# Last softmax sums on TensorE, slot 1's tokens gathered during attention, and four smaller moves

## The chip, the core and the metric

The kernel runs on one NeuronCore of one Trainium2 chip. The metric is the device time of one execution, in microseconds (us). The core's engines run side by side and wait for each other through semaphores: TensorE (PE: matmuls; its weight loads are listed as PEld), VectorE (DVE), ScalarE (ACT), GpSimd (POOL), and SyncE (SP), which here only issues DMAs. POOL issues the DMAs that gather or scatter rows by an index (DMA_INDIRECT).

## What is computed

Attention with normalized q and k, and behind it a mixture of experts that sends each token to one expert. Cut to what matters:

```python
# 8 batches, 12 heads, 448 tokens, head size 64
q_n, k_n = rmsnorm(q, g_q), rmsnorm(k, g_k)
scores = (q_n @ k_n.T) / 8
attn = exp(scores - max) ; attn = attn / (sum(attn) + 1e-9)
x = (attn @ v) laid out as 3584 tokens x 768

logits = x @ w_gate + modality_bias[modality_id]      # 8 experts
e_idx = argmax(logits, axis=1)
gate_w = softmax(logits)[arange, e_idx]
for e in range(8):
    mask = e_idx == e
    h = relu(x[mask] @ w1[e])                          # 768 -> 1024
    out[mask] = gate_w[mask] * (h @ w2[e])             # 1024 -> 768
```

## The kernel before

**Attention.** The work is cut into 48 units; unit u holds two heads (h = 0, 1) of batch u // 6. A unit has seven steps j, and the counter n = 7 u + j runs from -22 (a run-in) to 335. At each step the table `PLAN` says which pieces each engine gets. The scores of step j are the matmuls `st`; ACT's exponential turns them into the tiles p[:, j]; the matmuls `av` multiply p with v. Step 3 holds both heads (64 partitions each), the steps 0 to 2 the one head, 4 to 6 the other. `avcopy` takes the finished unit out of PSUM, DVE transposes it, and it is stored to `x_d` in DRAM.

The softmax's denominators take two stages. `csum` (line 924) adds the seven p tiles of a unit into two tiles `cs`, one for each head: one SCALAR_TENSOR_TENSOR on DVE and five 128x448 additions on POOL. `sums` (line 970) then adds over the partitions with four matmuls, against a table `sel` of zeros and ones, for two units at once. `gates` multiplies the same tokens with w_gate, into the same PSUM tile `pm`, and `recips` and the routing functions pick each token's expert and its place in that expert's list. `route_put` writes the list rows to `l_d` in DRAM, one scattered DMA for each of a batch's four chunks (c = 0 to 3).

**Mixture of experts.** The lists are cut into 14 static slots of 256 tokens. A slot has 24 steps. In the first eight, 144 matmuls `ph` (line 550) multiply the slot's tokens with w1, in four groups of 36 (`ph_0` to `ph_3`); in the other sixteen, 96 matmuls `py` (line 581) do the second product. Every fp32 operand is split in a high and a low part, so each product is three matmuls. ACT casts the high part, DVE subtracts it to get the low part:

- x: POOL gathers the rows of a slot in eight DMAs (`xrw<-x_d,i`, the function `xload`); DVE scales and transposes them, in three groups (`xtr`); ACT casts (`xcp`) and DVE subtracts (`xw<-xrw,xw`);
- w1: three gathers into `r_0`, `r_1`, `r_2`, and twelve pieces (`w1w<-r,w1w` 128x512). `ph_0` wants the pieces 0, 4 and 8, `ph_1` the pieces 1, 5, 9, and so on;
- w2: four gathers into `r2w`, and four pieces (`w2lw<-r2w,w2ha` or `w2hb`);
- the hidden layer: `hhw` (ACT) and `hlw` (DVE) empty each `ph` group from PSUM. There are two PSUM tiles for `ph`, so `ph_2` can't start before `hlw` has emptied `ph_0`.

The table `MOE` gives the step for each piece; what it doesn't name stands at a step that a formula gives. Slots 0 to 2 are tabled from the lists of the first six batches and can start while the last two are still in attention; the rest are tabled (`tables2`, the small DVE operations `tb_...`, `nbp`, `nbi`) when all batches are routed. The last part of attention and the start of the experts are woven by hand: between the two halves of `ph_0` stand the last `av`, `sums` and `gates`.

Nothing reorders work at run time: each engine works through its list in the order written, and waits where a semaphore isn't there yet. Nearly all instructions are issued through the recording helper at lines 54 and 55, so those two line numbers say nothing; the tiles' names do. `xrw` and `r2w` are large buffers that several things use in turn.

Of the kernel before, what the change touches and what calls it, by code (L numbers as in the profile page):

```python
# [68 lines left out]
def kernel(  # L69
# [36 lines left out]
    wg = cp.tile([128, NP, 32], F32, name="wg")  # L106
    sel = cp.tile([128, 2, 32], F32, name="sel")
# [12 lines left out]
    V.memset(lnb[:, 1:2], -22.0 * math.log(2.0))  # L120
    V.memset(wg, 0.0)
    V.memset(sel, 0.0)
    for i in range(2):
        V.memset(sel[:, i, 16 + i : 17 + i], 1.0)

    def load_gains():
        SY.dma_start(gg[:, 0], g_q.unsqueeze(0))
        SY.dma_start(gg[:, 1], g_k.unsqueeze(0))

    def gain_product(ps):  # L130
        for i in range(2):
# [1430 lines left out]
```

## Time and profile before

| | |
|---|---|
| time, three runs | 1060.64, 1062.4, 1065.34 us (median 1062.4) |
| the profiled execution | 1063.27 us, its span 1061.5 us |
| mean granted TensorE clock | 0.977 of full |
| busy, of the span | PE 95%, PEld 75%, DVE 73%, POOL 69%, ACT 66% |
| matmuls `ph` / `py` / `st` | 255.6 / 115.0 / 175.0 us and more for other shapes |

The profiled execution lies 0.87 us above the median and 1.77 us above its own span. Attention ends at about 552 us of the span, the experts take the rest. Busy shares are means over stretches with different limits, so they don't say what any one stretch waits for.

### The profile page before, as it was taken

Reading aid. Unit: us, or ns where it says so; the run is one execution under the profiler, and the core shown is the slowest. Engines: PE = TensorE matmul, PEld = TensorE weight load, DVE = VectorE, ACT = ScalarE, POOL = GpSimd, SP = SyncE. Lnnn points to the kernel's source line nnn. Section 1 sums busy time; section 2 is a strip of 40 time slices with the busy share of each in tenths; the row PEclk is TensorE's granted clock in tenths of the full one; section 3 lists DMA queues with packets and bytes.
Section 4 is the critical chain, followed back from the end, with each engine's and each line's share of the span. In section 5 each row is a group of like instructions: output and inputs, shape, how many; then the busy total and the mean of one; then the engine's idle time right before and its main releaser. Section 6 shows DMA issues by size and latency. Waiting matters only on the chain. (4 is left out here: it accounts for less than half of the span.)

```text
span 1061.5 us, 19477 instructions
## 1 busy us (share of the span) xinstructions
PE 1006.8 (95%) x6271; PEld 800.8 (75%) x6271; DVE 778.5 (73%) x1500; ACT 698.0 (66%) x1409; POOL 729.7 (69%) x743
## 2 busy tenths in 40 slices
PE   7789999999999999998979799999999999999996
PEld 6646565665566656554549699999999999999996
DVE  7778887887888888887696786766766677566830
ACT  5668998888888888876554445545645555455630
POOL 4697877898888888887765766776556655566231
PEclk8999999999999999999989798999999999999999
DMA  6767777767677776656613112221172211121070
GB/s 178 159 185 191 189 187 189 185 168 178 173 191 187 183 186 166 163 141 154 191 48 123 50 44 46 62 65 48 35 265 76 63 32 43 49 61 45 32 256 33
DMA packets 174803, 133.30 MB, mean 126 GB/s; under 512 B 119148, under 2 KB 168400, under 8 KB 173540
## 3 DMA queue, kind: packets, MB, share of 16 engines
q1 hardware_dynamic: 150836, 90.69, 35.0%
q0 software_dynamic: 23856, 41.28, 12.2%
q8 instruction: 51, 0.84, 0.4%
q14 instruction: 60, 0.49, 0.2%
HBM read 139.06 MB, written 24.18 MB: 154 GB/s over the span
## 5 line engine op out<-in xcount | busy, mean ns | idle before, releaser
L550 PE MATMUL ph<-xw,w1w 128*128 128x256 f32 x2016 | 255.6, 289 | 9.7 <-ACT xw L54 5.5
L550 PEld LDWEIGHTS ph<-xw,w1w 128*128 128x128 f32 x2016 | 251.3, 197 | 14.7 <-ACT xw L54 6.3
L54 DVE TENSOR_REDUCE at_hlw<-sa 128x1 f32<-128x448 f32 x336 | 204.7, 613 | 78.1 <-PE sa L889 63.0
L916 PE MATMUL st<-w1w 128*128 128x448 f32 x480 | 175.0, 414 | 11.9 <-ACT at_w2lw L54 10.4
L916 PEld LDWEIGHTS st<-w1w 128*128 128x128 f32 x480 | 84.1, 191 | 102.2 <-ACT xw L54 24.9
L54 POOL DMA_INDIRECT xrw<-x_d,i x112 | 135.6, 1210 | 36.6 <-issue 30.6
L54 POOL DMA_INDIRECT r2w<-in_moe_w_dram,tb_w2i x48 | 55.9, 1164 | 107.7 <-DVE w2lw L54 101.9
L54 DVE TENSOR_TENSOR w1w<-r,w1w 128x512 fp32r<-128x512 f32 (+1 forms) x180 | 113.9, 679 | 16.2 <-ACT w1w L54 16.2
L889 PE MATMUL sa<-w1w 128*128 128x448 f32 x282 | 107.8, 384 | 10.1 <-DVE at_hlw L54 9.3
L54 ACT ACTIVATE at_w2lw<-st 128x448 f32<-128x448 f32 x168 | 89.6, 541 | 39.2 <-PE st L916 34.9
L581 PE MATMUL py<-w2lw,hhw 128*128 128x384 f32 x448 | 115.0, 334 | 0.0
L54 ACT ACTIVATE hhw<-ph 128x512 fp32r<-128x512 f32 x56 | 33.5, 598 | 119.9 <-PE ph L550 119.9
L54 ACT CAST w1w<-xw 64x448 fp32r<-64x448 f32 x188 | 105.5, 561 | 6.1 <-DVE xw L54 2.4
L54 ACT CAST w1w<-r 128x512 fp32r<-128x512 f32 (+1 forms) x180 | 102.8, 639 | 1.7 <-ACT w2hb L54 1.0
L916 PE MATMUL st<-w1w,w2ha 65*128 65x448 f32 x288 | 101.1, 371 | 1.2 <-DMA w1w<-xw 1.2
L54 ACT ACTIVATE r2w<-st 128x448 f32<-128x448 f32 x168 | 90.1, 539 | 16.5 <-PE st L916 10.7
L54 DVE TENSOR_TENSOR w2lw<-r2w,w2ha 128x1536 fp32r<-128x1536 f32 x28 | 49.2, 1758 | 67.1 <-ACT w2ha L54 63.7
L54 POOL TENSOR_TENSOR xrw<-r,at_hlw 112x512 f32<-112x512 f32 x89 | 93.6, 1053 | 5.4 <-PE tr L802 3.5
L54 POOL TENSOR_TENSOR r2w<-r2w 128x448 f32<-128x448 f32 (+1 forms) x72 | 84.2, 1170 | 15.5 <-ACT r2w L54 6.6
L54 ACT ACTIVATE yw<-py,lt 128x384 f32<-128x384 f32 x55 | 29.0, 577 | 81.7 <-issue 56.8
L581 PEld LDWEIGHTS py<-w2lw,hhw 128*128 128x128 f32 x448 | 81.0, 188 | 0.0
L889 PEld LDWEIGHTS sa<-w1w 128*128 128x128 f32 x282 | 54.0, 192 | 23.7 <-DVE at_hlw L54 18.0
(312 smaller groups left out, 2140.9 us busy)
## 6 DMA issues: line engine op xcount, KB each, us to landing
w1w<-xw SPq DMA_DIRECT2D x312, 112.0 KB
r<-in_q_dram SPq DMA_DIRECT2D x48, 224.0 KB
r<-in_k_dram SPq DMA_DIRECT2D x48, 224.0 KB
w2ha<-xw SPq DMA_DIRECT2D x72, 112.0 KB
x_d<-at_w2hb SPq DMA_DIRECT2D x8, 672.0 KB
x_d<-yw SPq DMA_DIRECT2D x8, 672.0 KB
r2w<-in_v_dram SPq DMA_DIRECT2D x24, 128.0 KB
at_w2lw<-in_v_dram SPq DMA_DIRECT2D x24, 128.0 KB
```

What stands on the lines that cost most here:

```text
L54: return fn(*a, **kw)
L550: PE.matmul(ps[:, i], lhsT=lt_, rhs=rt_[:, c], start=n == 0, stop=n == 17)
L581: PE.matmul(ps[n][:, :384], lhsT=lt_[:, j, 128 * t : 128 * t + 128], rhs=rt_[:, 384 * n : 384 * n + 384], start=j == 0 and m == 0, stop=j ...
L889: PE.matmul(ps[:, :S], lhsT=t["qq"][:, h, a : a + 128], rhs=t["kk"][h], start=True, stop=True)
L916: PE.matmul(ps[:, :S], lhsT=l, rhs=t["qq"][:, h] if first else t["ql"][:, h], start=first and (j != 3 or h == 0), stop=not first and (j != ...
```

## The change

1. **Sums.** For the units 46 and 47 `csum` is left out. A new function `psums` adds p over steps and partitions in one go, with eight matmuls a unit against a table `selw`: unit 46's in pairs between the last `st`, unit 47's where `sums` stood.
2. **Slot 1's x.** Its list rows and its eight gathers are issued in attention (n = 302, 314, 325 to 332). Its transposes move from the steps 16, 17, 19 to 8, 8, 12. Slot 2's gathers stand together at step 8 (five stood at 20, three at 32), its transposes at 26, 28, 30 (38, 40, 42). The last three units' `xt` moves out of `xrw`; for that w2's fourth piece of slot 0 is gathered at step 5, behind the last transpose.
3. **Lists.** `route_put` writes through 32 views of `l_d` that are told apart, so that the scattered writes don't wait for each other. The puts of batch 6 and 7 and the second tables (`rpos` step 14 to 8, `tab2` 21 to 9, `flush` 46 to 40) come earlier.
4. **Gate tables.** Six DMAs (w_gate in four, modality ids, bias) are issued by ACT at n = -22, no longer by SyncE at n = -2.
5. **Smaller.** `l_d` is zeroed by four DMAs (n = 8, 11, 14, 17), not eight (7 to 14); POOL's last addition for head 0 stands behind that of head 1's second (`cse`); the norms of load 4 move from n = 2 to 1, the squares of unit 6's k from 1 to 3. Many other entries of `MOE` change, most of them to what the formula gives anyway; from slot 5 on the order is the same but for one x group.

```diff
-'cse': (1, 2) ... ('sk', 6): 1 ... ('nk', 4): 2 ... 'lg': -2, 'lz': 7 ... 'x0': 28
+'cse': (2, 2) ... ('sk', 6): 3 ... ('nk', 4): 1 ... 'lg': -22, 'lz': (8, 11, 14, 17) ... 'x0': 27 ...
+ 'pj': (2, 3, 4, 6, 2, 3, 4) ... 'g1': 34, 'f1': 22, 'x1': (325, 326, 327, 328, 329, 330, 331, 332)
...
+    l_v = dram_disjoint_views(l_d[:], B * NCH)
...
-                    SY.dma_start(wg[64 * h : 64 * h + 64, i::2, 8 * h : 8 * h + 8], src[i, h ^ i])
-            SY.dma_start(modr, mod_id.bitcast(I32).rearrange("(b p w) -> p b w", b=B, p=CP))
+                    A.dma_start(wg[64 * h : 64 * h + 64, i::2, 8 * h : 8 * h + 8], src[i, h ^ i])
+            A.dma_start(modr, mod_id.bitcast(I32).rearrange("(b p w) -> p b w", b=B, p=CP))
...
-    xt_e = [view(xrw, 2 * DM + S * i, 128, S) for i in range(3)]
+    xt_e = [view(r2w, PW + VW + W, 128, S), xt_b[3], view(r2w, PW + VW + S, 128, S)]
...
+        def psums(u, js):
+            i = 2 * (u % 2)
+            for j in js:
+                for h in range(2):
+                    if j == 3 or j // 4 == h:
+                        k_ = i + (h ^ (u % 2))
+                        PE.matmul(pm[32 * k_ : 32 * k_ + 32, :S], lhsT=selh[h] if j == 3 else sel[1],
+                                  rhs=T[u]["p"][:, j], start=False, stop=False, tile_position=(0, 32 * k_))
...
-            G.indirect_dma_start(out=l_d[:], out_offset=IOFF(ap=posi[:, c : c + 1], axis=0),
+            G.indirect_dma_start(out=l_v[NCH * b + c], out_offset=IOFF(ap=posi[:, c : c + 1], axis=0),
...
-        XSTEPS = {0: ((1, 7, range(8)), (2, 17, range(5))), 1: ((2, 32, range(5, 8)),),
+        XSTEPS = {0: ((2, 8, range(8)),), 1: (),
...
+        for j in range(NJ):
+            put(NJ * (NU - 1) + P["pj"][j], "psums", NU - 2, ORD[0][j : j + 1])
...
-            if 0 <= i < NU and j in CSJ:
+            if 0 <= i < NU - 2 and j in CSJ:
...
+            if n in P["x1"]:
+                xload(1, [b_ for b_ in range(8) if P["x1"][b_] == n])
...
-                wload(0, 1)
+                wload(0, 1, (0, 1, 2))
...
+            if s == 0:
+                on(("w2", 0, 3), 5, part(wload, 0, 1, (3,)))
...
-        step(1, part(mm1_half, 0, 0, 1, p0), part(sums, u - 1), part(gates, g))
+        step(1, part(mm1_half, 0, 0, 1, p0), part(psums, u, (0, 4, 1, 5, 2, 6, 3)), part(gates, g))
```

Three places show what moves on the engines. The first is PE's list at the end of attention, from the last `av` of unit 46 to the gates; `pm` is the PSUM tile of sums and gates. Before:

```order
L916 MATMUL st_4_6332<-w1w 128x448 x2
L916 MATMUL st_2_6341<-w1w 128x448 x2
L1055 MATMUL rt_6345<-oh_6231,ones 128x32
L1056 MATMUL rt_6345<-oh_6231,tri 112x32
L916 MATMUL st_5_6354<-w1w 128x448 x2
L916 MATMUL st_6_6368<-w1w 128x448 x2
L550 MATMUL ph_0_6423<-xw,w1w 128x256 x18
L960 MATMUL av_6320<-at_w2lw 64x448 x6
L550 MATMUL ph_0_6423<-xw,w1w 128x256 x18
L975 MATMUL pm<-at_w2lw,sel 32x448 x2
L975 MATMUL pm<-at_w2hb,sel 32x448 x2
L982 MATMUL pm<-at_w2hb,wg 32x448
```

And with the change (line numbers are 5 to 15 higher):

```order
L990 MATMUL pm<-r2w,selw 32x448 x2
L921 MATMUL st_4_6356<-w1w 128x448 x2
L990 MATMUL pm<-r2w,selw 32x448 x2
L921 MATMUL st_2_6370<-w1w 128x448 x2
L990 MATMUL pm<-r2w,selw 32x448 x2
L1069 MATMUL rt_6376<-oh_6235,ones 128x32
L1070 MATMUL rt_6376<-oh_6235,tri 112x32
L921 MATMUL st_5_6384<-w1w 128x448 x2
L921 MATMUL st_6_6394<-w1w 128x448 x2
L990 MATMUL pm<-r2w,selw 32x448 x2
L555 MATMUL ph_0_6440<-xw,w1w 128x256 x18
L965 MATMUL av_6339<-at_w2lw 64x448 x6
```

Four pairs of `pm` matmuls now stand among `st` and in front of `ph_0`. Behind the second half of `ph_0`, where the two rows of `sums` stood, come the eight of unit 47:

```order
L555 MATMUL ph_0_6440<-xw,w1w 128x256 x18
L990 MATMUL pm<-at_w2lw,selw 32x448 x8
L996 MATMUL pm<-at_w2hb,wg 32x448
L996 MATMUL pm<-r2w,wg 32x448
L996 MATMUL pm<-at_w2lw,wg 32x448
L996 MATMUL pm<-r2w,wg 32x448
```

The second place is POOL's list from the last gathers of slot 0's x on: the ten additions of the units 46 and 47 before, and w2 and w1 behind them.

```order
L54 DMA xrw<-x_d,i_129 128x192 x2
L54 TENSOR_TENSOR r2w<-r2w 128x448
L54 TENSOR_TENSOR r2w<-r2w 64x448
L54 TENSOR_TENSOR at_w2lw<-r2w 128x448
L54 TENSOR_TENSOR r2w<-r2w 128x448
L54 TENSOR_TENSOR at_w2lw<-r2w 128x448
L54 TENSOR_TENSOR r2w<-at_w2lw 128x448
L54 TENSOR_TENSOR r2w<-r2w,at_w2lw 64x448
L54 TENSOR_TENSOR at_w2hb<-r2w,at_w2lw 128x448
L54 TENSOR_TENSOR r2w<-r2w,at_w2lw 128x448
L54 TENSOR_TENSOR at_w2hb<-r2w,at_w2lw 128x448
L54 DMA r2w<-in_moe_w_dram,ta_w2i 128x1536 x4
```

With the change the eight gathers of slot 1's x stand there, in one row of ten with the last two of slot 0; the row `xrw` x8 further down is slot 2's x, where slot 1's x stood before.

```order
L55 DMA xrw<-x_d,i_130 128x192 x10
L55 DMA r2w<-in_moe_w_dram,ta_w2i 128x1536 x3
L55 DMA r_0_153<-in_moe_w_dram,ta_w1i 128x2048
L55 DMA r_1_154<-in_moe_w_dram,ta_w1i 128x2048
L55 DMA l_d<-ltb,posi_6381 28672x16 x3
L55 DMA r_2_155<-in_moe_w_dram,ta_w1i 128x2048
L55 DMA r2w<-in_moe_w_dram,ta_w2i 128x1536 x3
L55 DMA xrw<-x_d,i_130 128x192 x8
L55 DMA r2w<-in_moe_w_dram,ta_w2i 128x1536 x2
```

The third place is DVE's list behind the last `hlw` of slot 0, while PE is in slot 0's `py`. Before, the w1 pieces and the placing of batch 7 (`bs`, `zb`, `px_e`) come first, and x's first group behind them:

```order
L54 TENSOR_TENSOR w1w<-r_0_152,w1w 128x2x256 x3
L54 TENSOR_TENSOR w1w<-r_1_153,w1w 128x2x256
L54 TENSOR_TENSOR w1w<-r_0_152,w1w 128x2x256
L54 TENSOR_TENSOR w1w<-r_2_154,w1w 128x2x256
L55 TENSOR_REDUCE bs_6773<-zb_119 128x40
L55 TENSOR_REDUCE zb_118<-bs_6773 128x8
L55 TENSOR_TENSOR px_e<-px_e,bs_6773 112x32
L55 TENSOR_TENSOR px_e<-px_e,oh_6570 112x32
L55 TENSOR_REDUCE px_e<-px_e 112x4
L55 CAST posi_6774<-px_e 112x4
L54 TENSOR_TENSOR xrw<-xrw,lt_128 128x8x64
L54 STREAM_TRANSPOSE xrw<-xrw 128x2x8x32
```

With the change two groups of x are scaled and transposed in front of the first w1 piece, and small operations stand between the pieces (further down those of `tables2`):

```order
L55 TENSOR_TENSOR w2lw<-r2w,w2hb 128x1536
L55 TENSOR_TENSOR xrw<-xrw,lt_129 128x8x64
L55 STREAM_TRANSPOSE xrw<-xrw 128x2x8x32
L55 TENSOR_TENSOR xrw<-xrw,lt_129 128x8x64
L55 STREAM_TRANSPOSE xrw<-xrw 128x2x8x32
L55 TENSOR_TENSOR w1w<-r_0_153,w1w 128x2x256
L56 TENSOR_REDUCE bs_6720<-zb_120 128x40
L56 TENSOR_REDUCE zb_119<-bs_6720 128x8
L56 TENSOR_TENSOR px_e<-px_e,bs_6720 112x32
L55 TENSOR_TENSOR xw<-xrw,xw 128x512 x2
L55 TENSOR_TENSOR w1w<-r_0_153,w1w 128x2x256
```

What moved: x to the front, and the small operations of the second tables from slot 1's `ph` into slot 0's `py`.

## Rows read from the trace of the kernel before

**Rows 1.** The chain that ended last, 560 to 720 us: start, length, what.

```profile
638.72 18.41 PE ph L550 x131
```

**Rows 2.** Stretches: length, busy time (x instructions) by engine, granted clock, DMA share, GB/s.

```profile
533.60:546.15 12.55, 7.46 (x36) 3.46 (x35) 11.80 (x15) 6.04 (x15) 8.01 (x7) 0.83 0.08 4
...
570.79:587.60 16.81, 16.81 (x98) 16.49 (x96) 8.94 (x17) 5.56 (x10) 13.76 (x11) 1.00 0.16 42
...
587.60:616.48 28.88, 22.50 (x145) 21.03 (x146) 24.94 (x54) 14.20 (x19) 21.79 (x18) 0.76 0.16 46
...
633.12:657.13 24.01, 21.26 (x146) 20.31 (x146) 16.03 (x22) 12.21 (x16) 13.49 (x11) 0.86 0.24 51
...
673.77:691.00 17.23, 17.23 (x145) 17.23 (x145) 12.75 (x17) 10.69 (x14) 12.84 (x11) 1.00 0.24 63
```

**Rows 3.** PE's timeline, 529 to 552 us: start, length, instruction, [idle before <-releaser].

```profile
530.34 0.55 PE L975 MATMUL pm<-at_hhw,sel 128*32 128x448 f32 x2
...
530.82 0.47 PE L916 MATMUL st<-w1w 128*128 128x448 f32 x1
...
533.61 2.48 PE L960 MATMUL av<-r2w,at_w2lw 128*64 128x448 f32 x12
...
540.62 0.68 PE L916 MATMUL st<-w1w 128*128 128x448 f32 x2 [2.40 <-ACT at_w2lw L54]
...
544.34 1.87 PE L916 MATMUL st<-w1w 128*128 128x448 f32 x4 [2.69 <-ACT at_w2lw L54]
...
546.15 2.96 PE L550 MATMUL ph<-xw,w1w 128*128 128x256 f32 x13
...
549.72 0.85 PE L550 MATMUL ph<-xw,w1w 128*128 128x256 f32 x5 [0.60 <-DVE xw L54]
```

**Rows 4.** DVE's timeline, 528 to 540 us.

```profile
529.70 0.42 DVE L54 TENSOR_TENSOR w1w<-r,w1w 128x256 fp32r<-128x256 f32 x1
...
531.22 1.88 DVE L54 TENSOR_TENSOR w1w<-r,w1w 128x256 fp32r<-128x256 f32 x1
...
533.35 1.24 DVE L54 SCALAR_TENSOR_TENSOR r2w<-r2w,half 128x448 f32<-128x448 f32 x1
...
537.07 1.63 DVE L54 TENSOR_TENSOR xrw<-xrw,lt 128x512 f32<-128x512 f32 x1
```

**Rows 5.** POOL's timeline, 528 to 538 us.

```profile
529.31 1.02 POOL L54 DMA_INDIRECT xrw<-x_d,i  x1 [0.16 <-issue]
...
531.65 2.45 POOL L54 TENSOR_TENSOR r2w<-r2w 128x448 f32<-128x448 f32 x2
```

**Rows 6.** ACT's timeline at 539 us.

```profile
539.48 0.65 ACT L54 CAST xw<-xrw 128x512 fp32r<-128x512 f32 x1 [4.46 <-DVE xrw L54]
```

**Rows 7.** DVE's timeline, 565 to 632 us.

```profile
565.89 1.72 DVE L54 TENSOR_TENSOR w2lw<-r2w,w2ha 128x1536 fp32r<-128x1536 f32 x1
...
589.13 0.69 DVE L54 TENSOR_TENSOR xrw<-xrw,lt 128x512 f32<-128x512 f32 x1 [9.26 <-DMA xrw<-x_d,i]
...
590.49 0.65 DVE L54 TENSOR_TENSOR w1w<-r,w1w 128x512 fp32r<-128x512 f32 x1
...
599.30 0.17 DVE L55 TENSOR_SCALAR nbi<-run 128x8 int32<-128x8 f32 x1
...
630.27 0.69 DVE L54 TENSOR_TENSOR xrw<-xrw,lt 128x512 f32<-128x512 f32 x1 [3.73 <-DMA xrw<-x_d,i]
```

**Rows 8.** PE's timeline, 587 to 617 us.

```profile
591.31 0.58 PE L550 MATMUL ph<-xw,w1w 128*128 128x256 f32 x1 [3.71 <-ACT xw L54]
...
598.60 18.04 PE L550 MATMUL ph<-xw,w1w 128*128 128x256 f32 x131 [0.41 <-DVE xw L54]
```

**Rows 9.** ACT's timeline at 9 us.

```profile
8.63 0.65 ACT L55 ACTIVATE at_hlw<-at_hlw,lnb 112x16 f32<-112x16 f32 x2 [4.19 <-DVE at_hlw L54]
```

**Rows 10.** SyncE's DMA queue at 36 us.

```profile
36.10 2.70 SPq L141 DMA_DIRECT2D wg<-in_moe_w_gate_dram  x4
```

**Rows 11.** POOL's timeline at 44 us.

```profile
43.90 2.28 POOL L54 TENSOR_TENSOR xrw<-xrw 112x256 f32<-112x256 f32 x5 [7.00 <-ACT xrw L54]
```

More of the change, by code (lines that the diff above doesn't have):

```diff
@@ L6 @@
 from concourse import mybir
+from concourse.ap import dram_disjoint_views
 from concourse.masks import make_identity
@@ L106 @@
     wg = cp.tile([128, NP, 32], F32, name="wg")
-    sel = cp.tile([128, 2, 32], F32, name="sel")
+    selw = cp.tile([128, 68], F32, name="selw")
     gs = cp.tile([128, 1], F32, name="gs")
@@ L121 @@
     V.memset(wg, 0.0)
-    V.memset(sel, 0.0)
-    for i in range(2):
-        V.memset(sel[:, i, 16 + i : 17 + i], 1.0)
+    V.memset(selw, 0.0)
+    V.memset(selw[:, 17:18], 1.0)
+    V.memset(selw[0:64, 35:36], 1.0)
+    V.memset(selw[64:128, 53:54], 1.0)
+    sel = [selw[:, 1:33], selw[:, 0:32]]
+    selh = [selw[:, 18:50], selw[:, 36:68]]
     def load_gains():
@@ L974, in sums @@
             for i in range(4):
-                PE.matmul(R[g][32 * i : 32 * i + 32, :S], lhsT=sel[:, m],
+                PE.matmul(R[g][32 * i : 32 * i + 32, :S], lhsT=sel[m],
                           rhs=T[u + i // 2]["cs"][:, i % 2 ^ i // 2], start=m == 0, stop=False,
                           tile_position=(0, 32 * i))
+        def psums(u, js):
[6 more added lines that the diff above has]
+                                  rhs=T[u]["p"][:, j], start=False, stop=False, tile_position=(0, 32 * k_))
         def gates(g):
@@ L1201 @@
             put(xt_at(u), "xt", u)
-            if u % 2:
+            if u % 2 and u < NU - 1:
                 put(NJ * (u + 1) + (SMJ if u < NP * (B - 2) else P["sml"]), "sums", u - 1)
@@ L1259 @@
                 sums(*a)
+            for a in todo.get("psums", ()):
+                psums(*a)
             for a in todo.get("gates", ()):
@@ L1310 @@
                 load_gate()
-            if 0 <= n - P["lz"] < LW // 2:
-                ZN = NE * NT // 8
-                SY.dma_start(l_d[ZN * (n - P["lz"]) : ZN * (n - P["lz"] + 1)].rearrange("(p r) w -> p (r w)", p=128), zt)
+            if n in P["lz"]:
+                ZN = NE * NT // len(P["lz"])
+                z_ = P["lz"].index(n)
+                SY.dma_start(l_d[ZN * z_ : ZN * (z_ + 1)].rearrange("(k p r) w -> p k (r w)", p=128, r=28),
+                             zt.unsqueeze(1).to_broadcast([128, 8 // len(P["lz"]), 28 * LW]))
             for h in range(3):
@@ L1321 @@
                 xload(0, (m // 2 - 1,))
+            if n == NJ * NU - P["g1"]:
+                for kind, f in deferred(lambda: state["get1"](1, 1, (0,))):
+                    f()
+            if n == NJ * NU - P["f1"]:
+                state["fin1"](1, 1, (0,))
+            if n in P["x1"]:
+                xload(1, [b_ for b_ in range(8) if P["x1"][b_] == n])
             if i >= NU - 2 and j < 6:
@@ L1359, in run_at @@
                 seen.add(w)
-        seen = set()
+        seen = {("x", 1, 0), ("fin", 1)}
         def NEED(w):
@@ L1373, in NEED @@
             if w[0] == "xcp": return [("xtr", *w[1:])]
-            if w[0] == "xtr": return [("x", w[1], bl[0]) for v in XS_ for w_, n_, bl in v if w_ == w[1]] + [("xtr", w[1], g_) for g_ in range(w[2])]
+            if w[0] == "xtr": return [("x", 1, 0)] * (w[1] == 1) + [("x", w[1], bl[0]) for v in XS_ for w_, n_, bl in v if w_ == w[1]] + [("xtr", w[1], g_) for g_ in range(w[2])]
             if w[0] == "w1":
@@ L1382, in NEED @@
             if w[0] == "s2": return [("w2", w[1], w[2])]
-            if w == "s2v": return [("s2a", w[1])]
+            if w[0] == "s2v": return [("s2a", w[1])]
+            if w == ("s2a", 3): return [("w2", 0, 3)]
             return []
@@ L1404 @@
         for s in range(1, NS1):
[L1405 to L1406 removed]
+            lists_at(("get", s), 0, lambda s=s: state["get1"](s, 1, (1,) if s == 1 else (0, 1)))
+            if s > 1:
+                lists_at(("fin", s), 4, lambda s=s: state["fin1"](s, 1, (0,)))
         lists_at("get0", 4, lambda: state["get1"](0, 1, (1,)))
@@ L1472 @@
         p0 = mm1_open(0, 2)
-        step(4, part(mm1_half, 0, 2, 0, p0), part(xt, u), lambda: None)
+        step(4, part(mm1_half, 0, 2, 0, p0), part(xt, u), lambda: seen.add("xtlast"))
         step(5, part(mm1_half, 0, 2, 1, p0))
```

11 lines of the change are left out of this document (5 added, 6 removed).

## The prediction

> **What bounds the kernel now.** The profiled execution took 1063.27 us (span 1061.5), 0.87 above the median 1062.4. I first read the chain of waits from its end backwards. From 638.72 us on it holds nothing but PE [rows 1]: 131 of a slot's 144 `ph`, then `py` and `ph` in turn, slot after slot. So a microsecond can be won only ahead of 638.72, and there only where PE waits or has half a clock. For that I cut the stretch from the last units to slot 2 into pieces by stage [rows 2]. A slot's `ph` take 17.23 us at full clock (the last row) and slot 0's `py` 16.81. But slot 1's `ph` took 28.88 us, 11.6 more, at a granted clock of 0.76; slot 2's took 24.01, 6.8 more, at 0.86. The end of attention, 12.55 us, has PE busy for 7.46 at 0.83. These three are what the change can reach, besides the run-in.
>
> Third, who ends the waits. At the end of attention ACT does, late with the exponentials, and ACT itself sat idle 4.46 us for DVE's transposed x [rows 3, 6]. In slot 1 PE waits for x, DVE having waited 9.26 us for the gather; in slot 2 DVE waited 3.73 us for the same [rows 7, 8].
>
> **Sums on TensorE.** POOL's ten additions of the last two units go. One takes about 1.2 us [rows 5], and DVE's two-input operations stretch beside it: a w1 piece of 128x256 takes 0.42 us beside a gather, 1.88 beside additions; a scaling of x takes 1.63, and 0.69 elsewhere [rows 4, 5, 7]. The gather beside which 0.42 was taken is of the kind that replaces the additions, so I count the four stretched operations from 531.22 to 537.07 as freed: 1.46 and 0.94 for the two outer ones, about 0.9 each (between them) for the two inner, and 1.2 for DVE's own share of `csum`, which goes too: 5.4 us in all. That is more than ACT's idle 4.46, so PE's waits of 2.40 and 2.69 us in front of `st` should go [rows 3, 6].
>
> The Trainium skill, "SBUF — State Buffer", section "SBUF: two separate sides", says that a VectorE operation with two SBUF inputs and a GpSimd operation that reads SBUF shut each other out for a whole instruction; this trace's 0.42 against 1.88 agrees with it.
>
> Into the freed time come unit 46's eight matmuls. No such row exists in this place; the nearest is `av`: 12 passes in 2.48 us, two column groups side by side, 0.41 a pass of both [rows 3]. An fp32 matmul is two passes here, so a pair is 0.82 us and four pairs 3.3 (6.6 if the groups don't run side by side). Changing between `sums` and `st` took 0.48 from start to start, 0.07 more than a pass [rows 3]; eight changes are 0.6. So 3.9 of the 5.1 us of waits are filled, 1.2 is gained. The first `ph` waits 0.60 less; its 18 matmuls, 3.81 us now, cost 2.2 at full clock (18/144 of 17.23): 1.6 more. Together 3.4. Unit 47 pays with 3.3 of its own, less the 0.8 of `sums` (two passes of four groups): 2.5 lost. Net **gain 0.9**; from -6 (groups in series) to +4 (all of it hidden).
>
> **Slot 1.** Its gathers run on POOL in place of the additions, eight of 1.02 us like the one beside attention [rows 5], where the additions took 1.2 each, and they start near 531.65, almost 40 us before slot 0's `py`: no cost. With x there, DVE's list decides. Let T be the start of slot 0's `py`. DVE finishes the last w2 piece near T + 3.7 (two of 1.7 behind `hlw`). Up to w1's piece 8, the first that PE can lack, stand nine pieces and three x subtractions at 0.61, three x groups at 1.36 (scaling to next operation), and some 23 small operations at 0.2, a few longer: 5.5 + 1.8 + 4.1 + 5.0 = 16.4 [rows 7]. So piece 8 is ready at T + 20.1. PE wants it after 16.8 of `py` and 12 `ph` (1.4): T + 18.2. Wait 1.9. Pieces 9 to 11 come by T + 24.8, in time. But 15 more small operations and one w2 piece (1.7) stand ahead of `hlw` for `ph_0`, near T + 31, and `ph_2` needs its PSUM tile near T + 28 at full clock: perhaps 1.5 more. In slot 2, rows show that a clock lost to a few waits costs more than the waits: 24.01 - 21.26 = 2.75 idle, but 6.8 lost, so 4.0 by the clock [rows 2]. With 3.4 of waits I take 3.2 for the clock here: 6.6 still lost of 11.6, **gain 5.0**. Ends: 0 and 11.6. As a cross-check, PE's last wait ended at 598.60, T + 27.8 [rows 8], and piece 8 comes 7.7 sooner.
>
> **Slot 2.** Its gathers leave at slot 0's step 8, eight of 1.02 [rows 5] from T on; the transposes that want them stand in slot 1's `ph`, T + 20 and later, so 10 us are left for the landing. The wait of 3.73 is gone, and with it all of the 6.8: **gain 6.7**. Lower end 3, if one x group still comes late and only the clock's share is halved.
>
> **Run-in.** SyncE's queue is rid of six issues, four of them 2.70 us [rows 10]; at that price all six are 4.05, in front of moves that units 1 and 2 wait for. ACT gets them where it sits idle 4.19 us for DVE [rows 9], so they are hidden by 0.1; if twice as dear there, 3.9 is lost. POOL's norms move out from behind an addition that waited 7.00 for ACT [rows 11]. **Gain 1.5**, between -3.9 and +3.
>
> **At nothing.** w2's fourth piece of slot 0 is gathered behind the last transposes, near 565.9 [rows 7]; PE wants it for the last quarter of the first half of `py`, T + 6.2 = 577, and cast and subtraction take up to 1.7 each: 7.7 us are left for issue and landing. Each us beyond is one of PE. The list views: POOL isn't on the path at that time. Four zeroing DMAs for eight, and `cse`: the same bytes and additions.
>
> **Sum.** 0.9 + 5.0 + 6.7 + 1.5 = 14.1. Against the profiled 1063.27: 1049.2; in terms of the median 1048.3. I say 1048.
>
> **Rivals.**
> *DVE stays the bound in slot 1.* The table operations now stand between the w1 pieces; if the pieces come no sooner than before, slot 1 gives nothing. For: DVE has 21 us of work in 16.8 of `py`. Against: it sat idle 9.26 of that time before. Time 1048 + 5 = 1053.
> *All waits go.* If the small operations are nearer 0.15, piece 8 comes in time and the clock never falls: 6.6 more, 1042. With the run-in's upper end 1040.
> *Changing the array's layout is dear.* If each of the eight changes costs a pass's full 0.55 rather than 0.07, and unit 47's two as well, 4.8 more: 1053. The Trainium skill, "TensorEngine Tiling (Array Packing)", "Key Properties", states that changing the tiling mode drains TensorE; this trace's 0.07 shows hardly any of it.
> *Slower.* The `tables2` operations decide: some 50 of them and of the placing stand in DVE's list ahead of slot 1's second half. At 0.2 us they fit. At 0.4 each 10 us come on top; PE would wait about that much longer for the pieces and for `hlw`, stay at half clock through slot 1's `ph` (up to 17 over), and slot 2's splits start late as well, so its 6.7 stays lost: -14.1 + 10 + 5 + 6.7 = +7.6, 1070. It decides from 0.25 each on, if both slots' gains go with it. Against it: 0.17 in the one row [rows 7]; only the seven on 288 elements are certain to be longer.
> *It does nothing:* the gathers were hidden anyway, and PE waits for w1 alone: 1060. Against it stands 9.26.
>
> **How the numbers follow.** Forecast 0.45, all waits go 0.17, DVE bound 0.17, dear layout 0.08, nothing 0.07, slower 0.06. The range reaches from 1040 (the second) over 1053 and the slack of 3.9 in the run-in to 1057, which leaves out the last two and a little below. A measurement here tells about 0.5%, 5.3 us, from no change: the bound is 1057.1. Faster: all but the last two and a little of the third and fourth, 0.85; same 0.10; slower 0.05.
>
> **What would show it.** PE without waits over 1 us between 537 and 546, the `pm` pairs at 0.8 us; w1 pieces on DVE at 0.42 there; slot 1's `ph` at 22 to 25 us with one wait near its 13th matmul; slot 2's at 17.3 and full clock; slots from 3 on unchanged at 33.9. Wrong, if DVE waits for `xrw<-x_d` again, if `pm` pairs take 1.6, or if ACT's first `at_hlw` comes later than 8.7.

## The result, and the profile after

The changed kernel takes **1071.37 us** (median of 5 runs, 1070.62 to 1071.93), the kernel before 1062.4 us beside it (5 runs, 1060.64 to 1065.51): a ratio of 1.0076, 95% interval 1.0054 to 1.0098. By the ratio it is slower by 8.1 us, not faster by 14. The profiled execution has a span of 1070.1 us, 8.6 more than before. The working of the prediction found the waits it looked for, and they did shrink; the time was lost in places that it had called unchanged or free.

Where, is read from TensorE's timeline at landmarks that both kernels have: the twelve `av` of a unit, and the first `ph` and `py` of each slot. Start in us, before and after, each from one profiled execution:

| landmark | before | after | after is later by |
|---|---|---|---|
| `av`, unit 41 | 479.9 | 475.2 | -4.7 |
| `av`, unit 42 | 491.1 | 486.8 | -4.3 |
| `av`, unit 43 | 504.3 | 508.4 | +4.1 |
| `av`, unit 46 | 533.6 | 541.3 | +7.7 |
| slot 0, `py` | 570.8 | 577.0 | +6.2 |
| slot 1, `py` | 616.5 | 619.6 | +3.1 |
| slot 2, first `ph` | 633.1 | 636.3 | +3.2 |
| slot 2, `py` | 657.0 | 653.5 | -3.5 |
| slot 3, `py` | 690.9 | 695.5 | +4.6 |
| slot 4, `py` | 724.8 | 733.4 | +8.6 |

From there to the end nothing changes. So the profiles show three losses: 8.4 us from unit 42 to 43, 3.6 us from there to unit 46, and 12.1 us in slots 3 and 4; and four gains: 4.7 in the run-in, 1.5 at the end of attention, 3.1 in slot 1, 6.7 in slot 2.

The smaller of them are no larger than what one execution differs from another by. The changed kernel and eleven of the experiments below are the same program up to unit 41; they reach it between 475.2 and 479.9 us, 478.2 on average, and the profile above is the earliest of them. The stretch from unit 43 to 46 takes between 30.6 and 34.1 us in the four profiles (this one, a0, e1, e5) that are one program up to slot 3.

The stretches by stage, after (length, busy time of PE, PEld, DVE, ACT, POOL with counts, granted clock, DMA share, GB/s); they answer to [rows 2]:

```profile
495.40:503.57 8.17, 0.08 (x2) 0.01 (x1) 0.84 (x2) 1.13 (x2) 4.11 (x4) 0.69 0.58 145
503.57:508.35 4.78, 2.71 (x7) 1.57 (x7) 0.73 (x2) 1.59 (x3) 0.00 (x0) 0.50 1.08 225
508.35:512.64 4.29, 4.29 (x13) 1.25 (x13) 0.93 (x4) 0.32 (x2) 2.15 (x2) 0.55 0.33 69
541.28:552.12 10.84, 10.15 (x51) 3.54 (x51) 8.69 (x18) 7.61 (x18) 5.98 (x6) 1.00 0.27 62
577.00:594.00 17.00, 16.90 (x98) 16.59 (x97) 14.06 (x30) 6.87 (x11) 13.65 (x12) 1.00 0.28 85
594.00:619.60 25.60, 21.19 (x146) 20.26 (x145) 24.74 (x70) 13.06 (x19) 18.82 (x14) 0.87 0.14 35
636.30:653.50 17.20, 17.20 (x145) 17.20 (x144) 9.36 (x9) 8.30 (x9) 4.05 (x5) 1.00 0.11 26
670.40:695.50 25.10, 21.31 (x145) 20.21 (x146) 15.54 (x20) 10.54 (x13) 8.44 (x10) 0.86 0.12 26
712.10:733.40 21.30, 19.35 (x147) 18.95 (x146) 14.95 (x17) 9.17 (x11) 13.19 (x11) 0.92 0.20 53
```

The end of attention and slot 2 (the fourth row and the seventh) look as hoped: full clock, PE busy throughout. But in the first row PE does nothing for 8 us, and slots 3 and 4 (the last two rows), once at 17.3 us each, take 25.1 and 21.3. PE's timeline names what it waited for:

```profile
495.03 0.45 PE L921 MATMUL st<-w1w 128*128 128x448 f32 x1
503.57 0.74 PE L921 MATMUL st<-w1w,w2ha 65*128 65x448 f32 x1 [8.09 <-DMA w1w<-xw]
506.37 0.71 PE L894 MATMUL sa<-w1w 128*128 128x448 f32 x1 [2.06 <-DMA w1w<-xw]
...
508.35 4.36 PE L965 MATMUL av<-at_w2lw,r2w 128*64 128x448 f32 x12
...
536.11 0.96 PE L980 MATMUL pm<-at_w2hb,selw 128*32 128x448 f32 x2 [2.15 <-DVE lo L56]
...
676.49 19.16 PE L555 MATMUL ph<-xw,w1w 128*128 128x256 f32 x132 [1.77 <-ACT xw L55]
...
715.34 0.38 PE L555 MATMUL ph<-xw,w1w 128*128 128x256 f32 x1 [1.61 <-ACT xw L55]
```

**The loss at 500 us** is a wait for moves of normed data (`w1w<-xw`) that SyncE issues. Its queue shows why they came late; slot 0's list reads, then slot 1's, then the moves:

```profile
488.86 3.06 SPq L362 DMA_DIRECT2D lt<-l_d  x4
...
495.23 2.95 SPq L362 DMA_DIRECT2D lt<-l_d  x4
...
499.92 2.49 SPq L820 DMA_DIRECT2D w1w<-xw  x4
```

The second group is new there. Slot 0's reads are 3.84 us ahead of their place in the kernel before (492.70), the moves behind them only 0.12 (500.04): reads of small lists, 2.95 us of queue time, used up the lead. But PE's first matmul behind the moves started 2.5 us later than before (503.57 and 501.03), so the queue is not all. A second thing stands beside it: x0's gathers start a step later than before, so that GpSimd's second gather of slot 0's w1 now comes ahead of the first of them, at 498.62 instead of 506.32, and its traffic lies on that of the moves. In the kernel before, PE's waits at this place were short:

```profile
501.03 0.74 PE L916 MATMUL st<-w1w,w2ha 65*128 65x448 f32 x1 [1.22 <-DMA w1w<-xw]
502.34 0.71 PE L889 MATMUL sa<-w1w 128*128 128x448 f32 x1 [0.56 <-DMA w1w<-xw]
504.31 4.16 PE L960 MATMUL av<-at_w2lw,r2w 128*64 128x448 f32 x12
```

The waits account for the whole 8.4 us: 8.09 and 2.06 against 1.22 and 0.56. The twelve `av` behind them take 4.36 us where unit 46's took 2.48 [rows 3], at a granted clock of 0.55, that is mostly at the lower level of 1.2 GHz; but they took 4.16 here before as well, at 0.58, so the clock adds only 0.2 to the loss.

**The loss in slots 3 and 4** starts on VectorE, which waits for gathered x, and is explained by GpSimd's queue. VectorE, then GpSimd:

```profile
668.19 0.69 DVE L55 TENSOR_TENSOR xrw<-xrw,lt 128x512 f32<-128x512 f32 x1 [3.25 <-DMA xrw<-x_d,i]
...
705.75 0.69 DVE L55 TENSOR_TENSOR xrw<-xrw,lt 128x512 f32<-128x512 f32 x1 [3.87 <-DMA xrw<-x_d,i]
```

```profile
640.81 1.02 POOL L55 DMA_INDIRECT r2w<-in_moe_w_dram,tb_w2i  x1 [2.10 <-DVE w2lw L55]
644.86 0.99 POOL L55 DMA_INDIRECT r2w<-in_moe_w_dram,tb_w2i  x1 [3.02 <-DVE w2lw L55]
649.18 0.99 POOL L55 DMA_INDIRECT r2w<-in_moe_w_dram,tb_w2i  x1 [3.33 <-DVE w2lw L55]
653.50 0.99 POOL L55 DMA_INDIRECT r2w<-in_moe_w_dram,tb_w2i  x1 [3.33 <-DVE t L56]
654.79 1.01 POOL L55 DMA_INDIRECT xrw<-x_d,i  x1 [0.30 <-issue]
```

Slot 3's x gathers stand behind all four w2 gathers, and each of these waits until VectorE has split the piece of the slot before whose place it takes. Slot 3's `ph` begin at 670.40, 15.6 us after the first x gather; before, that gather left at 650.90, 22.7 us ahead of its slot. The table of steps had lost its entries for the w2 pieces of slots 3 and 4, which put the x gathers between them.

### The profile page after: what moved, and what is told of

It reads as the page before. It is cut to its first block, busy times and chain, and to the rows that moved or that the text cites. A ratio compares the mean times of both kernels' runs of the same rounds, so it can differ in the third digit from the quotient of the medians.

```text
span 1070.1 us, 19508 instructions
## 1 busy us (share of the span) xinstructions
PE 1012.1 (95%) x6295; PEld 802.5 (75%) x6295; DVE 771.1 (72%) x1499; ACT 698.3 (65%) x1409; POOL 708.6 (66%) x733
## 4 chain that ended last, share of the span: by engine, by line
PE 72%; DVE 8%; issue 8%; ACT 5%; DMA 3%; POOL 3%; SPq 1%; POOLq 0%; DVEq 0%; ACTq 0%
PE ph L555 17%; PE py L586 16%; PE st L921 13%; PE av L965 12%; PE sa L894 4%; PE tr L807 3%; PE pm L980 2%; DVE at_hlw L55 2%; DMA w1w<-xw 1%; POOL xrw L55 1%; DVE w1w L55 1%; ACT w1w L55 1%; ACT xw L55 1%; ACT at_w2lw L55 1%; DVE xw L55 1%
## 5 line engine op out<-in xcount | busy, mean ns | idle before, releaser
L55 POOL DMA_INDIRECT xrw<-x_d,i x112 | 132.9, 1187 | 43.5 <-issue 42.1
L921 PEld LDWEIGHTS st<-w1w 128*128 128x128 f32 x480 | 84.1, 190 | 99.1 <-ACT xw L55 24.9
L55 POOL TENSOR_TENSOR r2w<-r2w 128x448 f32<-128x448 f32 (+1 forms) x69 | 80.6, 1170 | 29.8 <-DVE r2w L55 9.5
```

The source lines that it names most:

```text
L55: return fn(*a, **kw)
L921: PE.matmul(ps[:, :S], lhsT=l, rhs=t["qq"][:, h] if first else t["ql"][:, h], start=first and (j != 3 or h == 0), stop=not first and (j != ...
```

## The experiments

They came in four batches, each with the kernel before on the same chip. These three chips scattered more than the first one (the kernel before had medians of 1063.12 to 1069.01 us), so ratios to the kernel before are compared. e1 to e6, a0 and e8 ran on one of the three, e7 and e9 to e11 on another, e12 to e14 on the last. A profile is of one execution; those of e1, a0 and e2 lie 7.5, 4.8 and 3.5 us above their medians.

| kernel | ratio | 95% interval |
|---|---|---|
| changed kernel again (a0) | 1.0087 | 1.0054 to 1.0119 |
| e1 w2 entries of slots 3, 4 back | 1.0030 | 1.0005 to 1.0055 |
| e2 slot 1's list reads later | 1.0054 | 1.0022 to 1.0086 |
| e3 x0 a step earlier | 1.0122 | 1.0070 to 1.0173 |
| e4 before, with the new start alone | 1.0001 | 0.9967 to 1.0035 |
| e5 x of slots 3, 4 early | 1.0008 | 0.9979 to 1.0036 |
| e6 = e5 + e2 | 0.9947 | 0.9916 to 0.9978 |
| e8 = e6, additions a step earlier | 0.9952 | 0.9921 to 0.9983 |
| **e9 = e6, slot 3's transposes earlier** | **0.9896** | **0.9872 to 0.9921** |
| e7 = e9, sums off TensorE | 0.9960 | 0.9946 to 0.9975 |
| e11 = e9, no list views | 0.9905 | 0.9881 to 0.9929 |
| e13 = e9, x0 a step earlier | 0.9931 | 0.9902 to 0.9960 |
| e10 changed, old order of slots 0 to 4 | 0.9955 | 0.9932 to 0.9979 |
| e14 = e10, sums off TensorE | 0.9976 | 0.9945 to 1.0007 |
| e12 before, with the views alone | 0.9943 | 0.9918 to 0.9969 |

### Slots 3 and 4

**e1** puts back the old steps of eight w2 gathers:

```diff
+MOE = {('w2', 3, 0): 55, ('w2', 3, 1): 57, ('w2', 3, 2): 53, ('w2', 3, 3): 63, ('w2', 4, 0): 78, ('w2', 4, 1): 81, ('w2', 4, 2): 81, ('w2', 4, 3): 85, ...
```

> The changed kernel with eight entries of the expert table put back, so that POOL gathers x of slots 3 and 4 between the pieces of the second matrix as in the kernel before, not behind all four; ten rows of POOL's order differ, nothing else. Theory (the place in POOL's queue): slot 3's first product, 25.3 us in the changed kernel, and slot 4's, 21.4, come back to about 17.3 each, so 12 us less: 1059 to 1060. Rival (the gathers are late because their lists are late, the attention being late): both stay long, 1069 to 1072.

Half of it held. Slot 4's `ph` fell to 18.1 us, slot 3's stayed at 24.0. Its x gathers still started only 18.4 us ahead of the slot (662.11 against 680.5), because the two w2 gathers left in front of them waited 10.46 us for VectorE. **e5** therefore moves the x gathers instead, behind the first w2 gather of slot 3:

```diff
-('x', 3, 0): 56, ('x', 4, 0): 67, ('x', 4, 3): 80
+('x', 3, 0): 48, ('x', 4, 0): 60, ('x', 4, 3): 61
```

> The eight x gathers of slot 3 go behind the first of slot 3's w2 gathers instead of behind the fourth, those of slot 4 right behind slot 3's w2 gathers; nothing else moves. Theory (the loss of 8.0 us in slot 3 and 4.1 us in slot 4 is the place of the x gathers in GpSimd's queue, behind w2 gathers that wait for VectorE): slot 3's gathers start about 12 us earlier, slots 3 and 4 fall back to 17 to 18 us each, and the time falls by 9 to 12 us, to 0.998 of the kernel before. Rival 1 (slot 3 is short of something else: DMA bandwidth, or its transposes' turn on TensorE): slot 3 stays at 23 to 25 us though its x is there, and the time changes by less than 5 us. Rival 2 (w2, now later behind the x gathers, takes over): slot 3's first matmuls fall to 17 us and the second matmuls of slot 3 wait the same 8 us for w2 instead.

The changed kernel itself was run again beside it:

> The changed kernel once more, as the base of the three edits beside it. By either theory it stands 0.76% above the kernel before (1.0054 to 1.0098), slot 3's first matmuls take about 25 us and slot 4's about 21 us instead of 17.3 us.

Its `ph` of slots 3 and 4 took 24.6 and 24.9 us. With the x early they took 20.5 and 18.1 (windows of e5):

```profile
677.30:697.80 20.50, 18.05 (x146) 17.45 (x145) 12.79 (x16) 9.25 (x11) 9.81 (x10) 1.00 0.19 51
714.50:732.60 18.10, 17.76 (x146) 17.39 (x145) 13.25 (x14) 8.85 (x10) 5.75 (x7) 1.00 0.12 25
```

The ratio falls by 0.79%, 8.4 us at this batch's 1068.96; the place in GpSimd's queue is the cause, and w2 did not take x's place as the thing waited for. Slot 3 keeps 3 us: its x gathers now start 28.0 us ahead of it (649.30), but its third transpose stands at step 68, among the subtractions of slot 4's w1. **e9** moves the transposes on top of e6 (below):

```diff
-xt_n = {2: (65, 66, 68),
+xt_n = {2: (64, 65, 66),
```

> Both repairs, and slot 3's three transposes of x at steps 64, 65 and 66 instead of 65, 66 and 68. Theory (the 3.5 us that slot 3 kept with its x early, 20.8 us against 17.3 us, are the third transpose, which stands behind the copies of slot 4's w1 at step 68 and ends at 675 us, 3.4 us after the slot's matmuls began): slot 3 falls to 17.3 to 18 us and the time by 2.5 to 3.5 us, to 0.992 of the kernel before. Rival (the copies of w1, now behind the transposes, take over): slot 3 stays near 20 us or slot 4 takes the 3 us.

Slot 3 has 17.3 us at full clock, slot 4 18.1 (windows of e9):

```profile
663.40:680.70 17.30, 17.30 (x147) 17.30 (x146) 11.29 (x14) 8.98 (x11) 10.77 (x10) 1.00 0.21 57
697.30:715.40 18.10, 17.76 (x147) 17.48 (x146) 13.27 (x14) 8.86 (x10) 5.79 (x7) 1.00 0.12 25
```

So the loss is found: of the 14.9 us that the two slots lost in a0, the order of the gathers gives back 10.9 and the transposes 3.2. The ratio fell by 0.51% from e6, 5.4 us, where slot 3 gives 3.5. The two ran on different chips, and in the profiles e6 reaches slot 0's `py` 8.0 us later than e9, where both are the same program (last section); so the transposes' own share of the 5.4 is not settled by the totals.

### The wait at 500 us

**e2** moves slot 1's list reads eight steps later, **e3** x0's gathers one step earlier, to their place in the kernel before (so that the w1 gather falls behind them), each alone. Both entries count steps back from the end of attention, so a larger number is an earlier step:

```diff
-'g1': 34        # e2
+'g1': 26
-'x0': 27        # e3
+'x0': 28
```

> The changed kernel with the reads of slot 1's list rows issued at step 310 instead of 302: behind three sets of moves between partition halves in SyncE's queue, not ahead of them. Theory (SyncE's queue): TensorE's waits of 8.1 and 2.1 us for those moves near 500 us shrink to 3 or less in all, 6 to 8 us less: 1063 to 1065. Rival (the moves land late because a 1 MB gather of the first matrix now runs beside them): the waits stay over 6 us, 1069 to 1072.

> The changed kernel with slot 0's gathers one step earlier, as before: POOL's gather of the first matrix's second third (1 MB) then stands behind the first of them again, which in the changed kernel waited 10 us. Theory (SyncE's queue alone): the waits for the moves near 500 us stay within 1 us of 10, time 1070 to 1072. Rival (the gather's traffic delays the moves): the waits shrink by 3 to 6 us, 1065 to 1068.

From unit 42's `av` to unit 43's it took 13.2 us before, 21.6 after, 14.3 in e2, 16.3 in e3. Both are causes: each alone gives back most of the 8.4, 7.3 us the reads, 5.3 the gather, and they overlap. The queue's part recurs: with the reads moved the stretch takes 11.7 to 14.3 us in e2, e6, e7 and e9, without 21.0 to 22.0 in a0, e1 and e5. For the gather there is the one profile of e3, so which part is larger stays open. In e2 PE has one wait for the moves left, and one for VectorE behind it:

```profile
501.82 0.47 PE L921 MATMUL st<-w1w,w2ha 65*128 65x448 f32 x1 [1.82 <-DMA w1w<-xw]
503.64 0.71 PE L894 MATMUL sa<-w1w 128*128 128x448 f32 x1 [1.35 <-DVE xw L55]
```

The totals follow only in part. e2's fell by 0.33% from a0, 3.5 us where 6 to 8 were expected, and that of e3 rose by 0.35%; both intervals overlap a0's. **e6** joins e2's edit to e5's, and **e8** also puts the additions of the sums a step earlier again (`'cse': (1, 2)`):

> The x gathers of slots 3 and 4 early, and slot 1's list reads eight steps later (n = 310 instead of 302), behind the moves of w1. Theory (two independent stalls, one in SP's queue at 500 us, one in GpSimd's at 655 us): both gains add up, 10 to 12 us in slots 3 and 4 and 6 to 7 us at 500 us; the time is 17 to 19 us below the changed kernel, 0.990 of the kernel before. Rival (what is gained at 500 us is lost behind it, since slot 1's x is late or the end of attention has another limit): the time is that of the x gathers alone, within 3 us.

> As the kernel with both repairs, and the last additions of the softmax sums one step earlier on GpSimd again, as before (cse 1, 2 instead of 2, 2), throughout attention. Theory (the 3.7 us lost at 530 to 541 us, where TensorE waited 2.15 us for VectorE's subtractions, come from unit 45's additions standing later, among the gathers of x): 2 to 4 us below the kernel with both repairs. Rival (those additions are no cost, the stall follows from the gathers of x0 standing a step earlier): within 1 us of the kernel with both repairs.

The queue's gain adds up with that of slots 3 and 4: 0.61% below e5, 6.5 us; with both e6 stands 15.0 us below a0, where 17 to 19 were expected. The place of the additions is worth nothing (0.9947 against 0.9952), so my guess on the 3.6 us lost ahead of unit 46 falls. **e13** tries x0's step on e9. The texts on record for e8, e10 and e13 have its direction turned round; as in e3, the step is an earlier one, the place of before:

> The kernel of the three repairs with x0's gathers one step later again, as before, so that the second w1 gather comes behind them. Theory (that gather's 1 MB beside the moves of w1 costs TensorE the rest of its waits for the moves, 0.56 and 3.02 us): these waits fall to 1 to 2 us and the time by 1 to 2 us. Rival (x0 and the w1 pieces behind it, a step later, cost more at the end of attention than the moves gain): 2 us or more above the kernel of the three repairs.

This settles nothing on the total. The waits for moves are gone from the profile (e9 still has one of 0.56 and one of 3.02 us), and in e3 the same step cut them from 10.15 us in all to 4.93, so the gather does bear on the moves; the Trainium skill, "DMA: Bandwidth & Descriptors", section "Issuing engines are not separate DMA queues", says that transfers started by different engines share the same 16 DMA engines, and here the trace is in keeping with it. The ratio is 0.35% worse, but the intervals overlap, and e13 ran on another chip than e9. Up to unit 46 its profile lies 2.6 us ahead of e9's; it loses 8.8 behind it, where ScalarE stands idle as described in the last section. Which step is the better one for x0 stays open.

### The sums, the views, the order, the start

**e7** takes from e9 the sums by TensorE: units 46 and 47 get GpSimd's and VectorE's additions and the old pairs of matmuls again.

```diff
-            if 0 <= i < NU - 2 and j in CSJ:
+            if 0 <= i < NU and j in CSJ:
-        step(1, ..., part(psums, u, (0, 4, 1, 5, 2, 6, 3)), part(gates, g))
+        step(1, ..., part(sums, u - 1), part(gates, g))
```

> The kernel of the three repairs with the sums of units 46 and 47 by GpSimd, VectorE and two pairs of matmuls again, as before. Theory (the sums by TensorE gain 0.9 to 1.5 us net: waits of 2.4 and 2.7 us against 22 matmuls): 1 to 4 us above the kernel of the three repairs, and the waits for these sums are back. Rival (GpSimd's additions, now in the middle of slot 1's gathers, delay them and VectorE's subtractions): over 5 us above it. Second rival (the sums are worth nothing, since what waits for them is off the path): within 1 us.

It costs 0.64%, 6.8 us, seven times the 0.9 predicted and with intervals apart: the first rival. VectorE and GpSimd in e7 at 552 us show how:

```profile
551.72 4.61 DVE L55 TENSOR_TENSOR w1w<-r,w1w 128x256 fp32r<-128x256 f32 x1
```

```profile
551.38 2.49 POOL L55 TENSOR_TENSOR r2w<-r2w,at_w2lw 64x448 f32<-64x448 f32 x2
553.84 2.20 POOL L55 TENSOR_TENSOR at_w2hb<-r2w,at_w2lw 128x448 f32<-128x448 f32 x2
```

A subtraction of 0.4 us takes 4.61: it ends 0.3 us behind the fourth of four additions. The x split queued behind it comes late by as much, and PE waits for it:

```profile
556.98 1.44 PE L555 MATMUL ph<-xw,w1w 128*128 128x256 f32 x5 [4.96 <-DVE xw L55]
```

With slot 1's eight gathers ahead of them on GpSimd, the additions slide into this place. **e10** has the old order of slots 0 to 4 (the old table of steps, slot 1's lists, gathers and transposes, and the old places of the last units' outputs and w2's fourth piece), **e14** is e10 with e7's edit:

> The changed kernel with the order of slots 0 to 4 of before: slot 1's lists, x gathers, transposes and weights where they stood, the table of steps of before, units 46 and 47's outputs and the fourth w2 piece in their old places. What stays of the change: the sums by TensorE, the gate tables by ScalarE, the list views, the four zeroings, x0 one step earlier. Theory (the moved order of slots 0 to 4 costs as much as it gives: it gives 2.9 + 6.7 us in slots 1 and 2, takes 7.3 us at 500 us and 12 us in slots 3 and 4): about 10 us below the changed kernel, 0.998 of the kernel before, slots 3 and 4 at 17.3 us, slot 2 back at 24 us. Rival (the sums by TensorE or the earlier x0 cost time themselves): over 1.003 of the kernel before, with the loss ahead of slot 0.

> The changed kernel with the old order of slots 0 to 4, and the sums of units 46 and 47 by GpSimd and VectorE as before. Theory (the sums by TensorE are worth little by themselves, 0.9 to 1.5 us, and 6 us only where GpSimd's additions stand among slot 1's x gathers and lie beside VectorE's scaling of x): 1 to 2 us above the kernel with the old order and the sums by TensorE, 0.997 of the kernel before. Rival (the sums are worth 6 us in either order): 1.001 to 1.002 of the kernel before.

In the old order the sums are worth 0.21%, 2.2 us, within the intervals and across two chips: the prediction's 0.9 fits that order, not the new one. e10 also held a surprise. Slot 2's `ph` took 18.0 us in the old order too, where before they took 24.0 [rows 2]. Of the new things only the list views bear on that place, and **e12** gives the kernel before the views alone:

```diff
+    l_v = dram_disjoint_views(l_d[:], B * NCH)
-            G.indirect_dma_start(out=l_d[:], ...
+            G.indirect_dma_start(out=l_v[NCH * b + c], ...
```

> The kernel before with the list views told apart, and nothing else. Theory (with the old order of slots, slot 2's loss of 6 to 7 us came from the list writes on GpSimd that waited for each other, 1.93 + 0.58 + 1.38 us, and held back slot 2's last x gathers behind them; the views alone give it back): slot 2's first matmuls fall from 24 to about 18 us, VectorE's wait for slot 2's x is gone, and the time is 0.994 of the kernel before. Rival (the views are worth nothing; in the kernel with the old order slot 2 was mended by something else of the change): slot 2 stays at 24 us and the time within 0.2%.

It is 0.57% faster than before, 6.1 us, with slot 2's `ph` at 18.9 us, 5 less: most of what I had put down to slot 2's moved gathers. (In its profile 1.4 of the 5 is lost again in slot 2's `py`, and the rest of the gain stands ahead of slot 0's `py`.) List writes on GpSimd in the kernel before, and in e12:

```profile
594.28 1.38 POOL L54 DMA_INDIRECT l_d<-ltb,posi  x1 [1.93 <-DMA l_d<-ltb,posi]
...
618.54 0.94 POOL L54 DMA_INDIRECT l_d<-ltb,posi  x1 [1.38 <-DMA l_d<-ltb,posi]
```

```profile
589.46 1.03 POOL L55 DMA_INDIRECT l_d<-ltb,posi  x1 [0.30 <-issue]
...
612.31 0.94 POOL L55 DMA_INDIRECT l_d<-ltb,posi  x1 [0.30 <-issue]
```

Each write waited for the one before to land, and slot 2's last x gathers stood behind them. VectorE's 3.73 us for them [rows 7] are gone in e12. In the new order, where x leaves ahead of most list writes, the views are worth nothing, as **e11** (e9 without them) shows:

> The kernel of the three repairs with the eight list writes as one tensor again, so that each waits for the one before. Theory (GpSimd isn't on the path when the lists are written; the views are worth nothing by themselves): within 2 us of the kernel of the three repairs. Rival (the lists are written 10 to 15 steps earlier now, among w1 and x gathers, so a waiting list write holds back the gathers behind it on GpSimd): 3 us or more above it, with the wait in slots 0 to 2.

**e4** is the kernel before with the gate tables on ScalarE and the two steps of k (`('sk', 6): 3`, `('nk', 4): 1`) of the change:

> The kernel before with the run-in's edits alone: gate tables issued by ScalarE at the start, the two entries of the load order. Theory (all of the lead of 4.7 us that the changed kernel has at unit 40 comes from here and holds to the end): 1057 to 1059. Rival (the lead is eaten by a later wait, as the lists and the moves stand where they stood): 1060 to 1063.

A lead was there (2.7 us at unit 41, 2.0 at slot 0's `ph`), the total did not move: in its profile the lead is given back in slots 2 to 4. The interval is 3.6 us either way, so a gain of 2 us isn't excluded.

**The best kernel** is e9: the change with three lines mended. It is 0.8 to 1.3% faster than the kernel before (ratio 0.9896, interval 0.9872 to 0.9921), some 11 us of 1062.4, on the one chip where it ran.

## Why the prediction was wrong

The forecast was 1048 with 5% on slower; it came out slower, by none of the mechanisms named.

- **"Slots from 3 on unchanged at 33.9"** is the step that failed, for 12.1 us. It was listed as a sign to look for and never worked out. The rows of GpSimd's new order were at hand; that slot 3's x now stood behind four waiting w2 gathers could be read there, and what w2 waits for in the trace. e5 and e9 settle it.
- **"Its gathers ... no cost"**, on slot 1, failed as well: the gathers themselves cost little, but their list reads passed into SyncE's queue ahead of moves that TensorE waits for. Only GpSimd's side was priced; SyncE's queue was looked at in the run-in alone. With the w1 gather that x0's step let ahead, 8.4 us (e2, e3, e6).
- **Run-in, gain 1.5**: 4.7 by unit 41 in the one profile, but the twelve reach it at 478.2 on average, against 479.9 and 479.0 in the kernel before and in e12, which has its run-in. So the size fits, and the 4.7 isn't shown. ACT's first `at_hlw` came at 8.83, later than the 8.7 named as a sign of being wrong, and yet units 1 and 2 started 0.9 and 2.6 us earlier than before. The step took a lead in the run-in for a lead at the end; e4, with a part of it, ends where the kernel before does.
- **Sums, gain 0.9**: the net change at that place is 1.5 and a pair of matmuls takes 0.87 us from start to start, where 0.82 was worked out; the rival of dear changes of the array's layout fell. In the old order the sums measure 2.2 (e10, e14). What was mis-sized is their worth beside slot 1's gathers, 6.8 by e7 (on one chip).
- **Slot 1, gain 5.0**: measured 3.1 (from slot 0's `py` to slot 1's 42.6 us; 40.8 to 42.6 in all profiles of the new order, 45.6 to 46.7 in those of the old). The place was right: PE's three waits there, 1.03, 1.14 and 2.11 us, are for pieces of w1, at a clock of 0.87; the wait for `hlw` did not come. The rival *Slower* named 1070, near the measured 1071, but by chance: its small operations at 0.4 us did not come true, most took 0.14 to 0.24.
- **Slot 2, gain 6.7**: 6.7, and full clock. But most of the same gain was to be had from the views, which I put **at nothing** ("POOL isn't on the path at that time"). e12 shows that in the kernel before it was.
- The 3.6 us between units 43 and 46 stay partly open. PE's one long wait there, 2.15 us for VectorE's list operations, does not recur in e9, but the stretch took 33.9 us there as in e10, against 29.3 before and 28.5 in e12; neither the additions' place (e8, 33.3) nor the sums (e14, 32.2) nor x0 (e13, 32.2) accounts for it alone. The old order has it too (e10, e14), so slot 1's gathers aren't needed for it; x0's step and the additions' place were not undone together. With 30.6 to 34.1 us for one program, single profiles can't settle it.
- The 1.5 at the end of attention are weak, too. From unit 46's `av` to slot 0's `py` it took 35.7 or 35.8 us in the profile after, e9, e10 and e11, 35.8 to 37.2 with the old sums in the old order (before, e4, e12, e14), and 41.0 to 44.5 in eight others (last section). e7 and e9 to e11 ran on one chip, without that; how much of their numbers holds on the others is open.

## What to carry to other kernels

When a transfer is moved, read the whole queue that it joins and the whole one that it leaves: what waits in front of it, and what then stands behind it, each with what it waits for in the trace. An item that leaves a table of steps is moved as much as one that is rewritten. And price a removed wait by what stands in the queue behind it, not by whether its engine is on the path: two edits may each be enough for one gain, and then it counts once.

## What the runs showed of the hardware

- VectorE's two-input operation was shut out through four GpSimd additions in a row, 4.61 us. The Trainium skill, "SBUF — State Buffer", section "SBUF: two separate sides", says that the shared pair is held for a whole instruction; that the next GpSimd instruction can get it again before a waiting VectorE operation is what e7 adds, in this one place. Before, additions let an operation of VectorE through after 1.24 to 1.88 us [rows 4].
- Four list reads of 8 KB or less hold SyncE's queue for 2.95 to 3.06 us, four moves of 112 KB for 2.42 to 2.49: in these rows the bytes don't decide how long a DMA holds the queue.
- The lower clock behind a wait hardly followed the wait's length: behind 1.78, 3.02 and 10.15 us of waits for moves (before, e9, after) the next twelve `av` took 4.16, 4.35 and 4.36 us, at granted clocks of 0.58, 0.57 and 0.55, instead of 2.48.
- In e2, e5, e6 and e13 ScalarE stood idle 7.3 to 7.6 us near 545 us for something that is in no timeline, in e1, e3 and e8 for shorter times (2.1 to 4.4 us). From unit 46's `av` to unit 47's it took 18.4 to 22.0 us in these seven and in a0, 13.2 in the profile after, e9, e10 and e11, and 15.5 to 16.9 in the kernel before, e4, e12 and e14. e6 and e9 are the same program up to slot 3, so between these two it is no effect of an edit; the eight ran on two chips, e9 to e11 on a third. What it was stays open. In e6, ACT and PE:

```profile
545.85 0.54 ACT L55 ACTIVATE at_w2lw<-st 128x448 f32<-128x448 f32 x1 [7.54 <-remote]
```

```profile
546.44 1.11 PE L921 MATMUL st<-w1w 128*128 128x448 f32 x2 [4.92 <-ACT at_w2lw L55]
```
